# Attention and routed experts on one Trainium2 core: part of a weight split moved to GpSimd, routing temporaries in PSUM, masks in 64-row pieces, and a new order of the attention pass

## The chip, the cores and the metric

The kernel runs on one core of one Trainium2 chip. The core has five engines, each with its own in-order queue of instructions: TensorE (PE in the profile; PEld is its weight load), VectorE (DVE), ScalarE (ACT), GpSimd (POOL) and SyncE (SP, which here only issues transfers). Engines wait for one another through semaphores. Transfers between HBM and on-chip memory run on 16 DMA engines. The metric is the device time of one execution in microseconds, as the median of several runs.

## What is computed

Eight batches of eight heads go through two attentions whose results are added: one on queries, keys and values averaged in groups of four (then repeated four times), one local, in which a position sees its three neighbours on each side. The sums are the 4608 tokens of a mixture of eight experts: each token goes to the expert with the largest logit.

```python
out_d = sm_attn(q_d, k_d, v_d)                 # means of 4 positions
mask = np.abs(pos[:, None] - pos[None, :]) < 4
x = repeat(out_d, 4) + softmax(where(mask, scores, -1e9)) @ v
logits = x @ w_gate
expert_idx = np.argmax(logits, axis=1)
y = np.maximum(x @ w1[e], 0.0) @ w2[e]         # e = expert_idx of the token
out = softmax(logits)[expert_idx] * y
```

## The kernel before

**Attention.** 32 pairs of heads (NP = 32) go through a software pipeline. A list, `PASS` (L860), holds some fifty steps with a lag each; pass i (L878) calls each step in that order for pair i minus its lag, and each call appends its instructions to the engines' queues. So the list sets the order of work on every engine. In one pass stand, for different pairs: `pool_qk`, `pool_qk2`, `pool_v`, `pool_v2` (POOL, means of four); `s_loc` (PE: two matmuls that put the mask into PSUM, then 40 small score matmuls on 64x64 quarters of the array); `max_loc`, `sub_loc`, `sums`, `norm` (DVE) and `exp_loc` (ACT), the local softmax; `s_d`, `max_d`, `max_scale`, `exp_d`, `norm_d`, the same for the averaged attention; `t_loc`, `t_d` (PE transposes) and `e_loc`, `e_d` (ACT, their copies); `pv_loc`, `pv_d` (PE), `out_d` (ACT) and `add_up` (DVE), which write the token rows XT. The score bank pS, the bank pD and the output bank pPV have one buffer each; transposes rotate over three banks pX.

**Routing.** Every fourth pass closes a group of four or five tiles of 128 tokens. `ra_mm` (PE) and `ra_lg` (ACT copy) make its logits, the `rb_` steps (a PE turn, then small DVE and ACT operations) its expert and gate, the `rc_` steps its row in the sorted buffer xs in DRAM. `x_row` (L498: PE transposes, ACT copy into one of 7 slots) makes a tile's rows, and `x_out` (`scatter`, L525: a POOL memset and an indirect transfer) writes them into xs. Lags before: ra, rb and the first half of rc 4 (the same pass), x_row 4, the rest of rc and x_out 5.

**First weight.** In passes 15 to 30 `w1_hi` and `w1_lo` split 256 columns per pass of the first expert's w1 into a rounded high part (ACT, L177) and the rest (DVE, L179).

**Transition.** At the end of pass 31 `x_load(0, 0)` (L903) reads the first 256 rows of expert 0 back from xs, and the next three 512 KB weight blocks are requested. Then follow what is left of the pipeline (`steps(NP)` to `steps(NP + 3)`) with, between them, `route_b` of the last pair of batches (nine tiles, like each pair), `x_rows` for its tiles 2 and 3 (L911, L912), `prep` (turns and splits the rows read, L913) and the first expert matmuls (L915); the last groups' routing and scatters; and from L960 the loop over the experts, which the diff does not touch.

**Constants.** cb (identity, triangle, mask, bf16) and cf (f32) are issued on ACT's queue at the start; `pad_first` (L510) writes padding into xs in passes 3 and 4, and in pass 3 also the zero rows zs (L516).

## Time and profile before

| | before |
|---|---|
| runs (us) | 667.58, 667.40, 663.36; median 667.4 |
| profiled execution (us) | 670.7, span 668.9 |
| busy share of the span | PE 95%, DVE 54%, ACT 52%, POOL 33% |
| granted TensorE clock, mean | 0.98 of full speed |
| passes 0 to 31 and what is left of them | about 5 to 216 us of the span |
| experts | about 216 to 669 us |

The shares are means over two very different stages. In the expert stage PE is busy nearly all the time; in the attention stage DVE and ACT are busy some nine tenths as well. A row of the timeline reads: start in us from the start of the span, duration in us, engine, line, operation, output and inputs, count, and in brackets how long the engine stood idle before it and what ended the wait.

### The profile page before, as it was taken

How to read it: one execution, taken by the hardware profiler on the slowest of the kernel's cores; microseconds unless marked ns; L12 is line 12 of the kernel's file. 1: busy time of each engine (PE TensorE's matmuls, PEld its weight loads, DVE VectorE, ACT ScalarE, POOL GpSimd, SP SyncE). 2: the span in 40 equal slices, each digit the busy share in tenths (PEclk: the TensorE clock that was granted, in tenths of full speed). 3: DMA queues.
4: the chain of work that ended last, by engine and by line, in shares of the span. 5: the costliest groups of instructions: out<-in, count | busy, mean ns of one | idle time of the engine just before them, and what ended most of it. 6: DMA issues, size and time to landing. Idle time of an engine off the chain costs nothing.

```text
span 668.9 us, 15757 instructions
## 1 busy us (share of the span) xinstructions
PE 635.3 (95%) x6160; PEld 517.7 (77%) x6163; DVE 362.1 (54%) x715; ACT 347.6 (52%) x941; POOL 218.0 (33%) x324
## 2 busy tenths in 40 slices
PE   8799999999997989999999999999999989999994
PEld 4577777777775969888888888888888878888873
DVE  5868789999884537273274056157128238115020
ACT  4769799999995525362363254344236145224120
POOL 6765697798770611101101111101110101110111
PEclk9979999999998989999999999999999989999998
DMA  8987888988944388275266238328328528110001
GB/s 281 267 234 222 258 283 238 297 287 251 267 155 128 142 236 237 75 184 180 67 169 195 66 98 219 108 87 210 108 71 229 175 76 205 50 45 1 32 19 39
DMA packets 66227, 108.53 MB, mean 162 GB/s; under 512 B 15388, under 2 KB 36524, under 8 KB 66112
## 3 DMA queue, kind: packets, MB, share of 16 engines
q1 hardware_dynamic: 59840, 87.62, 46.9%
q0 software_dynamic: 5984, 19.01, 7.7%
q8 instruction: 66, 1.08, 0.7%
q10 hardware_dynamic: 288, 0.42, 0.2%
q14 instruction: 49, 0.40, 0.2%
HBM read 86.98 MB, written 23.67 MB: 165 GB/s over the span
## 4 chain that ended last, share of the span: by engine, by line
PE 77%; issue 10%; DMA 4%; POOL 4%; DVE 2%; ACT 1%; POOLq 0%; another core or an unknown queue 0%; SPq 0%; DVEq 0%; ACTq 0%
PE p L653 8%; PE p L652 8%; PE p L654 8%; PE p L666 7%; PE p L668 7%; PE p L667 7%; PE pD L286 3%; PE pPV L338 3%; PE pS L232 3%; PE pX L323 3%; PE pX L310 3%; PE pPV L351 3%; PE pX L748 2%; PE pX L767 2%; PE pX L501 2%
## 5 line engine op out<-in xcount | busy, mean ns | idle before, releaser
L652 PE MATMUL p<-xh,w1h 128*128 128x512 f32 (+1 forms) x288 | 107.6, 374 | 4.2 <-issue 2.0
L673 POOL DMA_INDIRECT out_dram<-y,tix x39 | 37.9, 973 | 217.0 <-ACT y L685 205.7
L653 PE MATMUL p<-xl,w1h 128*128 128x512 f32 (+1 forms) x288 | 107.0, 371 | 0.8 <-DVE xl L600 0.8
L654 PE MATMUL p<-xh,w1l 128*128 128x512 f32 (+1 forms) x288 | 106.7, 370 | 0.0
L666 PE MATMUL p<-w2h,hh 128*128 128x512 f32 x256 | 101.2, 395 | 0.0
L667 PE MATMUL p<-w2l,hh 128*128 128x512 f32 x256 | 99.7, 390 | 0.6 <-DVE w2l L642 0.6
L668 PE MATMUL p<-w2h,hl 128*128 128x512 f32 x256 | 99.8, 390 | 0.0
L657 DVE SCALAR_TENSOR_TENSOR hl<-p,hh 128x512 fp32r<-128x512 f32 (+1 forms) x72 | 45.5, 632 | 98.3 <-ACT hh L656 97.5
L656 ACT ACTIVATE hh<-p 128x512 fp32r<-128x512 f32 (+1 forms) x72 | 39.6, 551 | 82.0 <-PE p L654 81.0
L685 ACT ACTIVATE y<-p,gi 128x512 f32<-128x512 f32 x32 | 22.1, 689 | 94.2 <-PE p L668 89.8
L652 PEld LDWEIGHTS p<-xh,w1h 128*128 128x128 f32 x288 | 55.7, 193 | 14.5 <-issue 2.7
L653 PEld LDWEIGHTS p<-xl,w1h 128*128 128x128 f32 x288 | 55.6, 193 | 9.7 <-DVE xl L600 0.9
L654 PEld LDWEIGHTS p<-xh,w1l 128*128 128x128 f32 x288 | 55.6, 193 | 9.0
L667 PEld LDWEIGHTS p<-w2l,hh 128*128 128x128 f32 x256 | 48.1, 188 | 10.5 <-DVE w2l L642 1.0
L668 PEld LDWEIGHTS p<-w2h,hl 128*128 128x128 f32 x256 | 48.0, 188 | 10.3
L666 PEld LDWEIGHTS p<-w2h,hh 128*128 128x128 f32 x256 | 48.1, 188 | 9.4
L179 DVE TENSOR_TENSOR w1l<-raw,w1h 128x512 fp32r<-128x512 f32 (+1 forms) x72 | 51.3, 712 | 0.8
L642 DVE TENSOR_TENSOR w2l<-raw,w2h 128x512 fp32r<-128x512 f32 x64 | 43.4, 681 | 2.2 <-DMA xs<-xr,ix 1.5
L600 DVE TENSOR_TENSOR xl<-pX,xh 128x512 fp32r<-128x512 f32 x38 | 24.7, 684 | 35.2 <-ACT xh L599 34.2
L213 POOL TENSOR_TENSOR vdt<-vd 72x512 f32<-72x512 f32 x32 | 41.1, 1283 | 2.4
L177 ACT ACTIVATE w1h<-raw 128x512 fp32r<-128x512 f32 (+1 forms) x72 | 41.6, 578 | 0.0
L202 POOL TENSOR_TENSOR qkt<-qk 128x576 f32<-128x576 f32 x32 | 36.8, 1148 | 14.3 <-DMA qk<-in_qk_dram 12.2
(149 smaller groups left out, 1242.5 us busy)
## 6 DMA issues: line engine op xcount, KB each, us to landing
raw<-in_w_dram SPq DMA_DIRECT2D x64, 512.0 KB
qk<-in_qk_dram SPq DMA_DIRECT2D x32, 583.0 KB
vw<-in_vw_dram SPq DMA_DIRECT2D x32, 320.0 KB
vd<-in_vd_dram SPq DMA_DIRECT2D x32, 288.0 KB
xrow<-xs SPq DMA_DIRECT2D x32, 192.0 KB
xrow<-xs SPq DMA_DIRECT2D x32, 128.0 KB
xs<-zs SPq DMA_DIRECT2D x6, 512.0 KB
xs<-pad SPq DMA_DIRECT2D x3, 257.0 KB
```

Source lines behind the costliest of these rows:

```text
L177: nc.scalar.activation(hi[:, s], src[:, s], AF.Copy)
L179: nc.vector.tensor_sub(lo[:, s], src[:, s], hi[:, s])
L213: nc.gpsimd.tensor_add(t2, v[:, 0:2], v[:, 2:4])
L642: nc.vector.tensor_sub(lo, src, hi)
L652: nc.tensor.matmul(p, wh[:, fs], xh[:, k, r], start=(k == 0), stop=False)
L653: nc.tensor.matmul(p, wh[:, fs], xl[:, k, r], start=False, stop=False)
L654: nc.tensor.matmul(p, wl[:, fs], xh[:, k, r], start=False, stop=(k == 3))
L656: nc.scalar.activation(hh[:, f, r], p, AF.Relu)
L657: nc.vector.scalar_tensor_tensor(hl[:, f, r], p, 0.0, hh[:, f, r], op0=OP.max, op1=OP.subtract)
L666: nc.tensor.matmul(p, hh, wh, start=(f == 0), stop=False)
L667: nc.tensor.matmul(p, hh, wl, start=False, stop=False)
L668: nc.tensor.matmul(p, hl, wh, start=False, stop=(f == 7))
```

## The change

1. `w1_lo` runs on GpSimd instead of VectorE (only there; the experts' later splits stay on VectorE). `rc_run`, the addition to the running counts, also goes to GpSimd.
2. The routing temporaries rd and rs are columns of the PSUM bank that `rb_turn` wrote, not SBUF tiles.
3. The mask stands twice in the constants, for both halves of the rows, and `s_loc` writes it with four matmuls on 64x64 quarters instead of two on the full array. The mask is a tile and a transfer of its own, cf is issued after the second pair's q and k, its first use is after pass 2, and zs is written in pass 12.
4. `PASS` has a new order and new lags: rb 5, rc and x_out 6, x_row 5, s_d and max_d 1, exp_loc 1, pool_qk2 -1, pool_v2 0, eps and both inv 2, e_d and one half each of e_loc and t_d 3.

```diff
-B_END = B_MASK + NC * KW
+B_END = B_MASK + 2 * NC * KW
...
+    maskb = p1.tile([128, B_END - B_MASK], BF, name="mask", bufs=1)
+    nc.scalar.dma_start(maskb, csb[:, B_MASK:])
+    load_qk(1)
     cf = consts.tile([128, C_END], F32, name="cf")
     nc.scalar.dma_start(cf, cst)
-    load_qk(1)
...
-                nc.vector.tensor_sub(lo[:, s], src[:, s], hi[:, s])
+                (nc.vector if part is None else nc.gpsimd).tensor_sub(lo[:, s], src[:, s], hi[:, s])
...
-        for s in range(2):
-            nc.tensor.matmul(p[:, s * 512:s * 512 + NC * KW], identb, maskb, start=True, stop=False,
-                             skip_group_check=True)
+        for t in range(2):
+            for s in range(2):
+                r, o = slice((s ^ t) * 64, (s ^ t) * 64 + 64), s * NC * KW
+                nc.tensor.matmul(p[t * 64:t * 64 + 64, s * 512:s * 512 + NC * KW], identb[r, r], maskb[r, o:o + NC * KW],
+                                 start=True, stop=False, skip_group_check=True)
...
-        d = RS[m, "d"] = rp.tile([128, 5, E], F32, name="rd", bufs=1)
+        d = RS[m, "d"] = RS[m, "p"][:, 256:296].rearrange("p (t e) -> p t e", e=E)
...
-        sc = RS[m, "sc"] = rp.tile([128, 5, E], F32, name="rs", bufs=1)
+        sc = RS[m, "sc"] = RS[m, "p"][:, 320:360].rearrange("p (t e) -> p t e", e=E)
...
-        nc.vector.tensor_add(crun, crun, RS[m, "cs"])
+        nc.gpsimd.tensor_add(crun, crun, RS[m, "cs"])
...
-        if e == 0:
-            nc.sync.dma_start(zs, pad)
...
     PASS = (
-        (pool_qk2, 0), (norm, 2), (s_loc, 0), (w1_hi, 0), (ra_mm, 4), (max_loc, 0), (max_scale, 1),
...
+        (rb_turn, 5), (pool_qk, -1), (e_loc0, 3), (s_d, 1), (e_d0, 3), (rb_max, 5), (w1_hi, 0), (eps, 2),
...
+        if i == 2:
+            nc.vector.tensor_copy(crun, cf[:, C_CAP:C_CAP + E])
+        if i == 12:
+            nc.sync.dma_start(zs, pad)
```

On POOL, a pass of the weight split that is also a routing pass, before. The names: qkt, qkd and vdt, vds are the two steps of the means, ix the row numbers, xs<-xr the scatter.

```order
L202 TENSOR_TENSOR qkt<-qk 128x576
L219 TENSOR_TENSOR vds<-vdt 72x256
L213 TENSOR_TENSOR vdt<-vd 72x512
L475 CAST ix<-pos 128x5
L527 MEMSET spacer 1x1
L528 DMA xs<-xr,ix 42112x514
L208 TENSOR_TENSOR qkd<-qkt 128x288
```

And of the change (w1l is the low part of the weight):

```order
L207 TENSOR_TENSOR qkt<-qk 128x576
L218 TENSOR_TENSOR vdt<-vd 72x512
L213 TENSOR_TENSOR qkd<-qkt 128x288
L482 CAST ix<-pos 128x5
L467 TENSOR_TENSOR crun<-crun,cs 128x8
L224 TENSOR_TENSOR vds<-vdt 72x256
L532 MEMSET spacer 1x1
L533 DMA xs<-xr,ix 42112x514
L184 TENSOR_TENSOR w1l_2499<-raw,w1h_2498 128x256
```

Two instructions are new in the queue, and each second step of a mean now has another operation between it and its first step.

On DVE, a routing pass before: the routing chain (rm, rd, rs) stands between `sums` (L255) and `sub_loc` (L249) of the same pass in which its logits were made.

```order
L245 TENSOR_REDUCE mx<-pS 128x10
L255 TENSOR_REDUCE smd<-A 128x10
L405 TENSOR_REDUCE rm<-pX 128x5
L410 TENSOR_TENSOR rd<-pX,rm 128x40
L420 SCALAR_TENSOR_TENSOR rs<-rd,cf 128x40
L249 TENSOR_TENSOR A<-pS,mx 128x2x5x64
```

After the change that chain comes one pass later than the logits, early in the pass, and `sub_loc` directly follows `max_loc`.

On POOL at the transition, of the change, with what each instruction waits for (DMAHW are transfers issued by SP, DMASW those issued by POOL); the first row belongs to tile 6 of the third pair of batches, the second scatter to tile 7, the third to tile 8:

```order
L533 DMA xs<-xr,ix 42112x514 [waits Activation_49]
L532 MEMSET spacer 1x1 [waits Pool_49]
L533 DMA xs<-xr,ix 42112x514 [waits DMAHW2_49,DMAHW6_49,DMAHW1_49,DMAHW7_49,DMAHW0_49,Activation_49]
L532 MEMSET spacer 1x1 [waits Pool_49]
L533 DMA xs<-xr,ix 42112x514 [waits DMASW3_49,Activation_49]
L588 CAST tix<-gi 128x2
```

On ACT at the same place, of the change: the two copies of `x_rows` for tiles 2 and 3 of the last pair of batches, then the high parts xh of the rows read back.

```order
L449 ACTIVATE gt<-gt 128x4 [waits DVE_49]
L510 ACTIVATE xr<-pX 128x4x4x32 [waits DMASW1_49,PE_49]
L510 ACTIVATE xr<-pX 128x4x4x32 [waits DMASW2_49,PE_49]
L604 ACTIVATE xh_4462<-p_4464 128x4x128 [waits DMAHW4_49,DMAHW3_49,DMAHW5_49,DMAHW2_49,DMAHW6_49,DMAHW0_49,DMAHW7_49,DVE_49,Pool_49]
L604 ACTIVATE xh_4462<-p_4466 128x4x128 [waits DVE_49]
```

Before, the scatters of tiles 7 and 8 stood ahead of `x_load` in the program, and `x_load` waited for them. With lag 6 they stand behind it: it waits for tile 6 alone, and the scatter of tile 7 waits for its five reads (4 of rows, 1 of gates).

## Rows read from the trace of the kernel before

**Rows 1.** Table of stretches: from:to, length, busy time of PE, PEld, DVE, ACT, POOL with counts, granted clock, DMA share, GB/s. Passes 12 to 14; passes 16 to 21; the ten us after the first long wait of PE.

```profile
75.80:92.16 16.36, 15.44 (x354) 12.26 (x354) 14.86 (x37) 14.74 (x56) 10.01 (x15) 1.00 0.66 195
99.49:136.17 36.68, 35.05 (x770) 28.20 (x769) 33.37 (x80) 33.90 (x126) 29.25 (x39) 1.00 0.90 268
...
30.00:40.00 10.00, 6.97 (x67) 5.18 (x66) 3.46 (x9) 3.62 (x13) 6.32 (x7) 0.55 0.96 251
```

**Rows 2.** Timeline of DVE, `sub_loc` of passes 7, 10, 11, 15 and 31.

```profile
49.15 0.81 DVE L249 TENSOR_TENSOR A<-pS,mx 128x640 f32<-128x640 f32 x1
...
66.08 0.81 DVE L249 TENSOR_TENSOR A<-pS,mx 128x640 f32<-128x640 f32 x1
...
75.80 0.81 DVE L249 TENSOR_TENSOR A<-pS,mx 128x640 f32<-128x640 f32 x1
...
99.49 0.81 DVE L249 TENSOR_TENSOR A<-pS,mx 128x640 f32<-128x640 f32 x1
...
194.75 0.81 DVE L249 TENSOR_TENSOR A<-pS,mx 128x640 f32<-128x640 f32 x1
```

**Rows 3.** Timeline of ACT, the first `exp_d` of two passes of the weight split that follow each other, with no wait over 0.1 us between.

```profile
110.01 0.38 ACT L300 ACTIVATE AD<-pD,mxd 128x144 f32<-128x144 f32 x1
...
115.38 0.37 ACT L300 ACTIVATE AD<-pD,mxd 128x144 f32<-128x144 f32 x1
```

**Rows 4.** The chain that ended last, pieces on PE in passes 7 to 9: start, us, line, count. The ra_mm of a routing pass, and one pass without it, whose pieces follow without a gap from 53.40 to 58.55.

```profile
45.91 1.05 PE pX L384 x32
...
53.40 0.80 PE pPV L338 x37
...
55.55 0.33 PE pX L310 x3
...
57.56 0.27 PE pS L226 x2
57.84 0.71 PE pS L232 x40
```

**Rows 5.** The instructions of L179 up to 210 us: duration in ns, least, median, most, then the first and last start.

```profile
L179 DVE TENSOR_TENSOR w1l<-raw,w1h x16: 412/824/1105, 98.9 to 189.2; 128x256 fp32r<-128x256 f32 x16
```

**Rows 6.** Timeline of POOL: the start of its pass 15; row numbers and scatter of a routing pass; one pass without a wait; the second scatter of a pass with two; the start of its last full pass.

```profile
95.22 0.67 POOL L208 TENSOR_TENSOR qkd<-qkt 128x288 f32<-128x288 f32 x1
...
107.56 0.19 POOL L475 CAST ix<-pos 128x4 int32<-128x4 f32 x1 [1.99 <-DVE pos L470]
...
108.39 1.00 POOL L528 DMA_INDIRECT xs<-xr,ix  x1 [0.61 <-POOL spacer L527]
...
114.79 0.67 POOL L208 TENSOR_TENSOR qkd<-qkt 128x288 f32<-128x288 f32 x1
115.54 1.15 POOL L202 TENSOR_TENSOR qkt<-qk 128x576 f32<-128x576 f32 x1
116.65 0.73 POOL L219 TENSOR_TENSOR vds<-vdt 72x256 f32<-72x256 f32 x1
117.46 1.33 POOL L213 TENSOR_TENSOR vdt<-vd 72x512 f32<-72x512 f32 x1
...
118.98 0.99 POOL L528 DMA_INDIRECT xs<-xr,ix  x1 [0.15 <-issue]
120.00 0.67 POOL L208 TENSOR_TENSOR qkd<-qkt 128x288 f32<-128x288 f32 x1
...
149.21 0.96 POOL L528 DMA_INDIRECT xs<-xr,ix  x1 [0.21 <-issue]
...
192.31 0.68 POOL L208 TENSOR_TENSOR qkd<-qkt 128x288 f32<-128x288 f32 x1
```

**Rows 7.** Timelines of PE, ACT and DVE in pass 11, a routing pass.

```profile
71.89 0.60 PE L384 MATMUL pX<-XT,wgt 128*32 128x128 f32 x10 [0.97 <-issue]
...
72.52 0.38 ACT L391 ACTIVATE lg<-pX 128x256 f32<-128x256 f32 x1 [1.76 <-PE pX L384]
...
74.50 0.20 DVE L405 TENSOR_REDUCE rm<-pX 128x5 f32<-128x40 f32 x1 [2.97 <-PE pX L399]
```

**Rows 8.** Timelines of PE and of SP's issues around the first long wait of PE.

```profile
33.03 1.22 PE L338 MATMUL pPV<-AT,vw 64*64 64x58 f32 x34 [3.90 <-issue]
...
20.61 0.43 SPq L516 DMA_DIRECT2D zs<-pad  x1
```

**Rows 9.** Timelines at the transition: the last two-tile scatter on POOL, SP's issues, the turn on DVE, the gates' cast on POOL, the high parts on ACT, and the last pair's `add_up` on DVE.

```profile
196.50 0.96 POOL L528 DMA_INDIRECT xs<-xr,ix  x1 [0.21 <-issue]
...
201.67 1.82 SPq L564 DMA_DIRECT2D xrow<-xs  x4
203.54 0.46 SPq L576 DMA_DIRECT2D gi<-xs  x1
204.09 1.44 SPq L161 DMA_DIRECT2D raw<-in_w_dram  x3
...
206.27 1.32 DVE L595 STREAM_TRANSPOSE p<-xrow 128x512 f32<-128x512 f32 x2 [2.09 <-DMA xrow<-xs]
...
206.46 0.19 POOL L583 CAST tix<-gi 128x2 int32<-128x2 f32 x1 [8.24 <-DMA gi<-xs]
...
207.08 1.14 ACT L599 ACTIVATE xh<-p 128x512 fp32r<-128x512 f32 x2 [1.69 <-POOL tix L583]
...
214.96 0.83 DVE L366 TENSOR_TENSOR XT<-pPV,outd 128x290 f32<-128x290 f32 x2 [1.02 <-ACT outd L355]
```

More of the change, by code (lines that the diff above doesn't have):

```diff
@@ L69, in constants @@
         c_, t = divmod(g, 2)
-        b[t * 64:t * 64 + QB, B_MASK + c_ * KW:B_MASK + (c_ + 1) * KW] = m
+        for x in range(2):
+            o = B_MASK + (x * NC + c_) * KW
+            r = (t ^ x) * 64
+            b[r:r + QB, o:o + KW] = m
     c[:, C_TOK:C_TOK + NT] = np.arange(128)[:, None] + 128 * np.arange(NT)[None, :]
@@ L860, in attention_moe_kernel @@
     PASS = (
-        (pool_qk2, 0), (norm, 2), (s_loc, 0), (w1_hi, 0), (ra_mm, 4), (max_loc, 0), (max_scale, 1),
-        (norm_d, 2), (pv_loc, 3), (ra_lg, 4), (exp_d, 1), (rb_turn, 4), (pv_d, 3), (sums, 1), (rb_max, 4),
-        (t_d1, 2), (rb_sub, 4), (out_d, 3), (rc_run, 5), (w1_lo, 0), (rb_top, 4), (pool_qk, -1), (e_d1, 2),
-        (sub_loc, 0), (rb_first, 4), (add_up, 3), (rb_hot, 4), (rc_pos, 5), (t_d0, 2), (rb_eps, 5), (e_d0, 2),
-        (t_loc0, 2), (rb_exp, 4), (s_d, 0), (pool_v2, 1), (rc_last, 5), (pool_v, 0), (t_loc1, 2), (eps, 1),
-        (rc_ix, 5), (inv_d, 1), (e_loc0, 2), (x_out, 5), (exp_loc, 0), (rc_cs, 4), (e_loc1, 2), (rb_gate, 4),
-        (x_row, 4), (rc_place, 4), (inv, 1), (max_d, 0), (rc_rk, 4),
+        (rb_turn, 5), (pool_qk, -1), (e_loc0, 3), (s_d, 1), (e_d0, 3), (rb_max, 5), (w1_hi, 0), (eps, 2),
+        (rc_cs, 6), (t_d1, 3), (exp_loc, 1), (rb_sub, 5), (rb_exp, 5), (e_d1, 3), (rb_top, 5), (max_d, 1),
+        (rc_place, 6), (inv, 2), (rc_rk, 6), (max_scale, 1), (x_row, 5), (inv_d, 2), (rb_first, 5), (s_loc, 0),
+        (norm, 2), (rb_hot, 5), (rc_pos, 6), (norm_d, 2), (pool_v, 0), (max_loc, 0), (pool_qk2, -1),
+        (exp_d, 1), (pv_loc, 3), (rb_gate, 5), (rc_ix, 6), (pv_d, 3), (t_loc1, 2), (ra_mm, 4), (t_loc0, 2),
+        (out_d, 3), (sub_loc, 0), (e_loc1, 2), (rc_run, 6), (pool_v2, 0), (sums, 1), (rb_eps, 5), (rc_last, 6),
+        (t_d0, 2), (x_out, 6), (add_up, 3), (w1_lo, 0), (ra_lg, 4),
     )
@@ L873, in steps @@
                 f(i - lag)
-    nc.vector.tensor_copy(crun, cf[:, C_CAP:C_CAP + E])
     load_vd(0)
```

6 lines of the change are left out of this document (3 added, 3 removed).

## The prediction

> **What bounds the kernel now.** I read the table of stretches first. PE's 95% hides two stages: in the experts PE has no gaps and the diff does not touch a row there, so whatever changes must come from the attention passes and from the transition that follows them. In the attention stage no engine is alone: in passes 16 to 21 DVE is busy 33.4 and ACT 33.9 of 36.7 us, and DMA 0.90 of it [rows 1]. So I took the timelines of each engine, pass by pass. `sub_loc` on DVE marks the passes: passes 7 to 14 take 50.3 us (49.15 to 99.49), 9.7 of them pass 11; passes 15 to 30 take 95.3 [rows 2]. Three things hold them up. (a) The routing chain: in pass 11 PE's logits, ACT's copy, PE's turn and DVE's `rb_max` follow one another within one pass, and since `rb_max` stands ahead of `sub_loc`, ACT stands 1.76 and DVE 2.97 us; 0.97 of that began with PE itself waiting for nothing the profile shows [rows 7]. (b) In passes 15 to 30 the split on DVE: 0.41 us at best, 0.82 in the median, 1.1 at most, so it loses time beside POOL [rows 5]. (c) POOL is nearly full there too: a pass without a wait takes 5.21 us (114.79 to 120.00), and what it has to spare goes in waits for row numbers, 1.99 us in one [rows 6]. Earlier, PE stands 3.90 us in pass 5 [rows 8], and runs the ten us around and after it at a granted 0.55, for the most part the lower of its two levels [rows 1].
>
> At the end the way leads through POOL: its last scatter ends at 197.46, `x_load` is issued 4.2 us later, the rows are on chip 4.6 us after that, and ACT makes their high parts at 207.08 [rows 9]. The last pair's work waits behind them.
>
> **The change, part by part.**
>
> *Zero rows and constants.* zs is 128 x 514 x 4 bytes = 263 KB, which leaves the stretch where DMA is 0.96 busy at 251 GB/s [rows 1] and where PE's long wait lies, 12 us after zs was issued [rows 8]: 1.05 us of transfer, so what comes behind arrives about 1.0 us earlier. Where zs goes, around 80 us, DMA is busy 0.66 [rows 1], which covers it; without that cover it is 1.0 again. The mask adds 80 KB (0.3 us at that rate) to the start, under the first pair's q and k; cf later and crun after pass 2 are needed only by the routing. Taken as 0. **-1.0 us.**
>
> *Passes 7 to 14: the new order.* Logits, turn and rank now lie a pass apart, so (a) goes; what is late next is the fullest engine. ACT is busy 14.74 us in three passes, 4.9 each [rows 1]. PE's pieces of one pass follow each other for 5.15 us (53.40 to 58.55), and a routing pass adds 1.05 for the logits [rows 4], a quarter of that per pass, and I put 0.1 for turn and rank. Masks: two full-array matmuls take 0.27 us; the 40 score matmuls, on the same four quarters that the mask is to use, take 0.71, 18 ns for 64 columns of f32, where the full array takes 0.33 for 3 x 128 columns, 55 ns for 64 [rows 4]. So quarters run about three at a time, and four of 320 columns cost 0.27/2 x 4/3 = 0.18: 0.1 saved; the ends are 0.13 (all four together) and 0.54 (one by one). PE then needs 5.05 + 0.26 + 0.1 = 5.4, the fullest. 8 x 5.4 = 43.2 against 50.3 gives -7.1; I give back 0.6 because PE's own wait of 0.97 [rows 7] can return. **-6.5 us**; ends -8 (4.9 + 0.4 a pass) and -3.2 (only pass 11 returns to the mean of the others).
>
> The page TensorEngine Tiling (Array Packing) of the Trainium skill, section Restrictions and Gotchas, says that different row tiles cannot use one PSUM bank at the same time, and the new masks do send both halves of the rows to each bank. By it two quarters at most would overlap, the masks would cost 0.27 as before, and the sum would be 0.8 us worse. The score matmuls do the same and overlap, so the trace does not bear this out.
>
> *Passes 15 to 30: the low half on POOL.* DVE loses 16 times 0.82 us; that is covered, since ACT (5.37 us from one pass to the next, 110.01 to 115.38 [rows 3]) and POOL now set the pace. POOL before: 95.22 to 192.31 = 97.1 us for these 16 passes [rows 6]. After: a pass without a wait is 5.21; in it two second steps wait 0.08 for their first steps, where unrelated neighbours overlap by 0.04, and the new order puts another operation between both, 2 x 0.12 saved: 4.97. The low half has no row on POOL: 128 x 288 strided takes 0.67, in proportion 0.60 for 256; 72 x 256 contiguous 0.73; 128 x 576, more than twice as long, 1.15 [rows 6]. The first and the last are the ends; I take 0.73, same count and form, less 0.04 of overlap. 16 x 5.66 = 90.6, two second scatters 2.5 (0.96 + 0.21 + 0.09), and in four routing passes 0.12 for ix, 0.2 for the counts (about ix's 0.19) and 0.61 before the scatter, 3.7: 96.8. **-0.3 us**; by the ends -2.4 and +6.4. The waits for row numbers turn into work.
>
> The GPSIMD Engine Reference of the Trainium skill, section Key points, calls VectorE structurally about twice as fast on elementwise work. Twice the 0.41 of the undisturbed split would be 0.82 instead of 0.73, 1.4 us more in all, 665.4 instead of the time below. No row has this shape on POOL.
>
> *Pass 31 on POOL.* Before 192.31 to 197.46 = 5.15, with qkd and two scatters [rows 6, 9]; after vdt, vds and one scatter, 1.25 + 0.7 + 1.25 = 3.2. **-2.0 us.** `x_load` is thus issued 1.0 + 6.5 + 0.3 + 2.0 = 9.8 us earlier.
>
> *The transition: a new wait.* Before, ACT makes xh 5.4 us after `x_load` (201.67 to 207.08). Now the scatter of tile 7 waits for the five reads, and in ACT's queue the copy of tile 3 into the same slot, which waits for that scatter, stands ahead of xh. That is 4.8 us until the gates have landed (206.46), 1.0 on POOL, 4.2 for the transfer (as from 197.46 to 201.67; the weight blocks issued at 204.09 share the queue), 0.5 for the copy: 10.5 [rows 9]. **+5.1 us.** Queued behind it are all of ACT's steps for the last two pairs, on DVE the low parts, on PE the last transposes.
>
> *Behind xh.* From xh to the last `add_up` it takes 8.7 us before (207.08 to 215.80 [rows 9]). With e_loc0, both e_d and a transpose one step later, some four ACT copies of 0.3 us (nearest: 0.38 [rows 7]) come in front of the last outputs, part of them under the first expert matmuls: +1.0, between 0 and +2; the counts on POOL ahead of the last scatters +0.2. **+1.2 us.** Routing temporaries in PSUM: a bank is held until `rb_hot`, but its next user waits for `norm` just ahead of that; 0, at most one 0.2 us operation per routing pass, 1.4 in all.
>
> **Sum**: -1.0 - 6.5 - 0.3 - 2.0 + 5.1 + 1.2 = -3.5. The profiled execution goes from 670.7 to 667.2; it lies 3.3 above the median of the runs, which goes from 667.4 to **663.9**.
>
> **Rivals.**
> 1. PE's long wait in pass 5 goes as well. For it: zs stood just ahead of the transfers that run late there. Against: the other padding and the loads stay, and DMA is still full. It would save the 3.9 us, and at a granted 0.55 with 6.97 us busy in ten [rows 1, 8] about 0.45 x 7 = 3.1; less the 1.0 already counted, and 0.5 since the next pair's q and k limit: 663.9 - 5.5 = 658.4.
> 2. Slower: POOL sets the end and the low half costs its upper end, 1.15. Then 16 x 0.42 = 6.7 us come on top: 670.6. It passes the time before from 0.73 + 3.5/16 = 0.95 on. For it: POOL has no spare time in these passes, and `x_load` hangs on its queue. Against: the two nearest rows in size [rows 6].
> 3. The order does not do what it should: passes 7 to 14 keep the pace that they have apart from pass 11. The gain there is 3.2 instead of 6.5: 667.2, no change. For it: one-buffered banks (pS, pD, pPV) tie DVE, PE and ACT in rings. Against: with the new lags most handovers go to the next pass.
>
> **How the numbers follow.** My sum 0.42, its own range 660 to 668 from the ends of the mask, the transition and what lies behind xh; rival 1 0.22; rival 2 0.14; rival 3 0.22. A measurement of this kernel tells about 1% from no change: faster is below 660.7, slower above 674.1. Faster: rival 1 and a fifth of my own case, 0.30. Slower: rival 2 where it meets rival 3 (670.6 + 3.3) or a longer wait at the transition, 0.12. Same: 0.58. The range 655 to 672 leaves out the upper part of rival 2 and the lower of rival 1.
>
> **What would show it.** Order: DVE's wait ahead of `rb_max` under 0.5 us and passes 7 to 14 near 5.4; if 5.8, rival 3. Split: L184 on POOL near 0.73, POOL without waits in passes 18 to 30, DVE idle about a fifth; the median tells rival 2. Masks: four in about 0.18. PE's first long wait about 1 us earlier at its end; if it is gone, rival 1. Transition: the scatter of tile 7 directly after the gates' landing, ACT idle some 5 us ahead of the copy of tile 3. If ACT does not stand there, the prediction is too high by up to 5 us; if POOL has waits in passes 18 to 30, the sum's POOL terms are not the ones that count.

## The result, and the profile after

| | before | after |
|---|---|---|
| median of 15 runs each (us) | 665.13 (662.20 to 668.13) | 672.31 (666.00 to 678.87) |
| ratio, with 95% interval | | 1.0087 (1.0057 to 1.0116) |
| profiled executions (us) | 670.7 | 678.4, and 674.1 in a second one |

The changed kernel is slower by 0.9%, where 663.9 us and no loss were forecast; 672.31 lies just above the range. Its runs scatter over 13 us, those of before over 6. Ratios here leave out runs in a disturbed state and medians do not, so the two can differ, most for the gap of 320 bytes below. The rows that follow are of the second profiled execution (run `a0_again`), since the first one took 6 us more than the median; where the first is shown, it is said. The two profiles, before and `a0_again`, differ by 3.5 us, the medians by 7.2: the profiled execution of before lies 5.6 us above the median of its 15 runs.

Two lines of its page, then the table of stretches from `sub_loc` to `sub_loc`, passes 7 to 14 and 15 to 30, of the kernel before and of the changed one (columns as in [rows 1]):

```profile
span 672.4 us, 15936 instructions
...
PE 632.3 (94%) x6227; PEld 515.4 (77%) x6227; DVE 352.2 (52%) x691; ACT 344.0 (51%) x941; POOL 225.7 (34%) x348
```

```profile
49.15:99.49 50.34, 47.53 (x1033) 37.67 (x1032) 41.34 (x97) 43.45 (x155) 35.53 (x48) 1.00 0.81 253
99.49:194.75 95.26, 91.55 (x2049) 73.48 (x2047) 88.48 (x203) 87.67 (x317) 78.94 (x102) 1.00 0.84 256
```

```profile
44.84:89.23 44.39, 42.55 (x1043) 35.23 (x1031) 39.45 (x93) 40.87 (x152) 33.43 (x45) 1.00 0.97 288
89.23:191.39 102.16, 91.92 (x2097) 75.05 (x2094) 79.65 (x185) 88.09 (x324) 89.39 (x125) 0.97 0.82 244
```

In passes 15 to 30 VectorE is relieved (79.7 us of work, 88.5 before) and POOL has taken over (89.4, 78.9 before). In passes 7 to 14 the DMA engines have gone from a share of 0.81 to 0.97. PE was busy 47.5 of 50.3 and 91.6 of 95.3 us before, 42.6 of 44.4 and 91.9 of 102.2 now: in passes 15 to 30 it has as much to do as before and stands idle 10.2 us instead of 3.7. The timeline of DVE, `sub_loc` (now L256) of passes 7, 15 and 31, against 49.15, 99.49 and 194.75 [rows 2]:

```profile
44.84 0.82 DVE L256 TENSOR_TENSOR A<-pS,mx 128x640 f32<-128x640 f32 x1
...
89.23 0.82 DVE L256 TENSOR_TENSOR A<-pS,mx 128x640 f32<-128x640 f32 x1
...
191.39 0.82 DVE L256 TENSOR_TENSOR A<-pS,mx 128x640 f32<-128x640 f32 x1
```

So 4.3 us are gained up to pass 7, 5.9 more in passes 7 to 14, and 6.9 are lost again in passes 15 to 30 (102.2 us against 95.3). At pass 31 the lead is 3.4 us.

**The transition.** Timelines of SP, POOL, ACT, PE and DVE (answers to [rows 9]): the reads of rows, the scatter of tile 7, the copies of tiles 2 and 3, xh, PE's next transposes, and the last `add_up`.

```profile
195.53 1.83 SPq L569 DMA_DIRECT2D xrow<-xs  x4
...
201.53 0.96 POOL L533 DMA_INDIRECT xs<-xr,ix  x1 [8.25 <-ACT gt L449]
...
201.77 0.60 ACT L510 ACTIVATE xr<-pX 128x512 f32<-128x512 f32 x1 [0.71 <-PE pX L508]
206.76 0.60 ACT L510 ACTIVATE xr<-pX 128x512 f32<-128x512 f32 x1 [4.39 <-DMA xs<-xr,ix]
207.25 1.08 ACT L604 ACTIVATE xh<-p 128x512 fp32r<-128x512 f32 x2
...
207.41 0.78 PE L330 MATMUL pX<-cf,AD 112*72 112x112 f32 x3 [3.87 <-ACT xr L510]
...
218.79 0.82 DVE L373 TENSOR_TENSOR XT<-pPV,outd 128x290 f32<-128x290 f32 x2 [1.96 <-ACT outd L362]
```

The read is issued 6.1 us earlier than before. Then ACT stands 4.39 us for the scatter of tile 7 out of the slot that the copy of tile 3 needs, and xh comes 11.7 us after the read, 5.4 before. From xh to the last `add_up` it takes 11.5 us, 7.9 before. The lead of 6.1 has become a lag of 3.8. The granted clock in that stretch, from the table of stretches:

```profile
200.00:205.00 5.00, 1.98 (x8) 1.21 (x8) 1.90 (x6) 0.85 (x3) 2.20 (x4) 0.61 1.02 387
205.00:210.00 5.00, 2.04 (x15) 1.32 (x19) 2.07 (x5) 2.71 (x8) 0.00 (x0) 0.50 0.09 30
210.00:215.00 5.00, 5.00 (x62) 4.47 (x59) 1.03 (x3) 2.17 (x6) 0.00 (x0) 0.52 0.00 0
```

PE was busy two fifths of 200 to 210 us. The granted clock fell within 200 to 205 us, and PE ran its next work at 0.5, the lower of its two levels.

**The experts.** From the last `add_up` to the end it takes 453.6 us (672.4 - 218.79), and 453.9 before. But the profile of before holds a stop of PE there that this one does not. Its row in PE's timeline, and the stretch of 515 to 565 us of before and then of after:

```profile
538.63 0.50 PE L652 MATMUL p<-xh,w1h 128*128 128x512 f32 x1 [1.99 <-issue]
```

```profile
515.00:565.00 50.00, 48.01 (x205) 39.26 (x204) 24.15 (x39) 19.44 (x36) 6.37 (x13) 0.97 0.56 161
```

```profile
515.00:565.00 50.00, 50.00 (x220) 41.09 (x220) 25.88 (x42) 22.38 (x42) 6.04 (x11) 1.00 0.65 167
```

Behind the stop the granted clock is lower for 3.4 us. Without both the experts have become slower, though the diff touches no row of theirs. Groups of PE by line and shape, 270 to 535 us (count, busy us, mean ns of one), before and after:

```profile
L666 PE MATMUL p<-w2h,hh 128*128 128x512 f32 x165 | 65.1, 395 | 0.0
L667 PE MATMUL p<-w2l,hh 128*128 128x512 f32 x165 | 64.2, 389 | 0.0
L652 PE MATMUL p<-xh,w1h 128*128 128x512 f32 x160 | 62.2, 389 | 0.0
```

```profile
L657 PE MATMUL p<-xh,w1h 128*128 128x512 f32 x160 | 62.8, 393 | 0.0
...
L671 PE MATMUL p<-w2h,hh 128*128 128x512 f32 x158 | 62.6, 396 | 0.0
L672 PE MATMUL p<-w2l,hh 128*128 128x512 f32 x158 | 61.7, 391 | 0.0
```

Four nanoseconds in 389 in the mean of w1, with no wait in any row. The mean mixes two kinds. The same line in the changed kernel, in an odd expert (281 to 322 us) and in the even one behind it (333 to 372 us):

```profile
L657 PE MATMUL p<-xh,w1h 128*128 128x512 f32 x32 | 12.6, 395 | 0.0
...
L657 PE MATMUL p<-xh,w1h 128*128 128x512 f32 x32 | 12.5, 389 | 0.0
```

These matmuls overlap in the rows, so their pace is read from start to start: 233.3 ns in an odd expert, 226.7 in an even one, and 226.7 in both before. The outputs' scatters show the same: between the same two of an odd expert 55.4 us passed before (358.25 to 413.61), 56.4 now; of an even one 51.7 and 52.0.

```profile
358.25 0.99 POOL L673 DMA_INDIRECT out_dram<-y,tix  x1 [4.27 <-ACT y L685]
...
413.61 0.99 POOL L673 DMA_INDIRECT out_dram<-y,tix  x1 [4.43 <-ACT y L685]
```

```profile
361.80 0.98 POOL L678 DMA_INDIRECT out_dram<-y,tix  x1 [4.31 <-ACT y L690]
...
418.24 0.98 POOL L678 DMA_INDIRECT out_dram<-y,tix  x1 [3.88 <-ACT y L690]
```

Four odd experts at 1.0 and three or four even ones at 0.3 are 4.9 to 5.2 us.

### The profile page after: what moved, and what is told of

It reads as the page before. It is cut to its first block, busy times and chain, and to the rows that moved or that the text cites. A ratio compares the mean times of both kernels' runs of the same rounds, so it can differ in the third digit from the quotient of the medians.

```text
span 676.7 us, 15933 instructions
## 1 busy us (share of the span) xinstructions
PE 630.7 (93%) x6224; PEld 515.4 (76%) x6227; DVE 351.6 (52%) x691; ACT 343.9 (51%) x941; POOL 226.2 (33%) x348
## 3 DMA queue, kind: packets, MB, share of 16 engines
q1 hardware_dynamic: 59840, 87.62, 46.8%
## 4 chain that ended last, share of the span: by engine, by line
PE 67%; issue 10%; DMA 9%; POOL 7%; ACT 2%; DVE 1%; SPq 1%; POOLq 0%; another core or an unknown queue 0%; ACTq 0%; DVEq 0%
PE p L658 8%; PE p L659 8%; PE p L657 8%; PE p L673 7%; PE p L671 7%; PE p L672 7%; DMA xs<-xr,ix 6%; PE pD L293 2%; POOL xs L533 2%; POOL vdt L218 2%; PE pX L317 2%; PE pX L330 2%; PE pX L772 2%; PE pX L753 2%; PE pPV L345 2%
## 5 line engine op out<-in xcount | busy, mean ns | idle before, releaser
L662 DVE SCALAR_TENSOR_TENSOR hl<-p,hh 128x512 fp32r<-128x512 f32 (+1 forms) x72 | 45.5, 632 | 95.8 <-ACT hh L661 95.3
L657 PEld LDWEIGHTS p<-xh,w1h 128*128 128x128 f32 x288 | 55.3, 192 | 11.6 <-ACT xh L604 1.5
L533 POOL DMA_INDIRECT xs<-xr,ix x36 | 36.5, 1014 | 30.8 <-ACT gt L449 8.1
L184 DVE TENSOR_TENSOR w1l<-raw,w1h 128x512 fp32r<-128x512 f32 x56 | 39.5, 705 | 0.8
```

The source lines that it names most:

```text
L533: ins = nc.gpsimd.indirect_dma_start(out=xs, out_offset=bass.IndirectOffsetOnAxis(ap=IDX[m, t], axis=0), in_=xr, in_offset=None)
L657: nc.tensor.matmul(p, wh[:, fs], xh[:, k, r], start=(k == 0), stop=False)
L662: nc.vector.scalar_tensor_tensor(hl[:, f, r], p, 0.0, hh[:, f, r], op0=OP.max, op1=OP.subtract)
```

## Experiments

All are edits of the changed kernel unless said otherwise. Medians of before drifted between 662.5 and 665.1 us over the groups of runs, so the ratio to before on the same chip (95% interval) is the figure to compare. The columns in us are of each run's one profile: `sub_loc` of pass 7 to that of pass 31, read of rows to xh, xh to the last `add_up`; the last column is the mean w1 matmul of odd and even experts in ns.

| run | edit | median us | ratio to before | 7 to 31 | read to xh | xh to last add_up | w1 ns |
|---|---|---|---|---|---|---|---|
| before | | | | 145.6 | 5.4 | 7.9 | 389 |
| a0_again | none | 672.25 | 1.0100 (1.0060, 1.0139) | 146.5 | 11.7 | 11.5 | 393 |
| e1_out_ahead | tiles 7, 8 scattered ahead of the read | 674.12 | 1.0122 (1.0087, 1.0157) | 145.1 | 9.0 | 11.0 | 393 |
| e2_nine | nine slots | 665.83 | 1.0023 (0.9986, 1.0059) | 145.5 | 8.4 | 11.7 | 393 |
| e3_old_order | old list of the pass | 670.31 | 1.0083 (1.0056, 1.0111) | 146.5 | 6.0 | 8.2 | 393 |
| f1_after_cb | cb at its old size | 668.15 | 1.0033 (0.9996, 1.0070) | 146.6 | 12.3 | 11.9 | 389 |
| f2_before_cb | before, mask out of cb | 674.75 | 1.0124 (1.0074, 1.0174) | 145.1 | 5.4 | 8.5 | 393 |
| f3_rows_later | nine slots, rows 2, 3 later | 668.23 | 1.0035 (1.0003, 1.0067) | 144.0 | 5.9 | 15.3 | 393 |
| f4_right_gap | nine slots, gap of 640 B | 662.12 | 0.9963 (0.9924, 1.0002) | 151.3 | 8.1 | 12.2 | 389 |
| g1_low_dve | f4, low half on VectorE | 666.88 | 1.0064 (1.0041, 1.0087) | 147.6 | 8.5 | 12.0 | 389 |
| g2_zeros_early | f4, zero rows in pass 3 | 659.74 | 0.9963 (0.9933, 0.9993) | 144.4 | 7.5 | 12.0 | 389 |
| g3_temps_sbuf | f4, temporaries in SBUF | 659.77 | 0.9949 (0.9924, 0.9974) | 142.2 | 6.3 | 12.3 | 389 |
| g4_drain | f4, old lags after pass 31 | 662.05 | 0.9990 (0.9962, 1.0017) | 139.0 | 8.4 | 10.4 | 389 |
| h1_best | f4 with g2, g3, g4 and the counts on VectorE | 660.94 | 0.9973 (0.9940, 1.0006) | 155.3 | 7.8 | 10.7 | 389 |
| h2_half_values | f4, half of the value loads | 651.36 | 0.9807 (0.9757, 0.9856) | 146.4 | 9.0 | 11.6 | 390 |
| h3_gap_320 | nine slots, gap of 320 B | 669.62 | 0.9980 (0.9930, 1.0029) | 146.1 | 9.0 | 11.6 | 392 |
| h4_old_order_cb | old list, cb at its old size | 663.83 | 1.0009 (0.9980, 1.0038) | 147.5 | 6.7 | 9.2 | 389 |

### The slots, the transition and the list

> The changed kernel once more, unaltered, as the base of the next three on the same chip. Median near 672.3 us, between 666 and 679 as in the runs seen. Its profile should again show the ACT copy of the token numbers (L490) waiting for a scatter every fourth pass, most of it (4.7 us in the first profile) near 80 us, and ACT's high parts xh some 12 us after the first read of rows is issued.

The median is the same, and the waits are smaller or gone. ACT's copy of the token numbers (L490) in the second profile, and in the first one, with what PE then waited for there (ACT and PE timelines):

```profile
80.47 0.20 ACT L490 COPY xr<-cf 128x5 f32<-128x5 f32 x1 [1.83 <-DMA xs<-xr,ix]
```

```profile
84.27 0.20 ACT L490 COPY xr<-cf 128x5 f32<-128x5 f32 x1 [4.71 <-DMA xs<-xr,ix]
...
84.88 1.11 PE L508 MATMUL pX<-cf,XT 128*128 128x128 f32 x4 [4.13 <-ACT AT L324]
```

The copy writes into the slots from which the last group's last tile is still being scattered. Of two executions of one program one, of 678.4 us, loses 4.7 us there and the other 1.8. This wait near 80 us stands in all six profiles with seven slots and the zero rows in pass 12 (1.2 to 4.7 us), with the new list or the old one, and in neither of the two with the zero rows in pass 3 (before, f2). In `a0_again` the zero rows are issued at 67.36 us and the scatter that ends the wait at 72.88. That the one delays the other was not tried alone.

```diff
+            x_out(NP - 6)
             x_load(0, 0)
...
-            if 0 <= i - lag < NP:
+            if 0 <= i - lag < NP and not (i == NP and f is x_out):
```

> The scatters of tiles 7 and 8 of the third pair of batches stand ahead of the first read of rows again, the rest as in the change. Theory (a wait at the transition, from the slots and the lag of the scatter): the read is issued some 2.5 us later (two scatters of 1.0 with 0.25 around each on POOL), but xh comes 5.4 us after it instead of 11.9: 672.3 - 6.5 + 2.5 = 668.3 us. Rival (the last two pairs' own work, or the low granted clock there, sets the end, and ACT's wait lies beside it): 671 to 673. The waits in the passes (L490) are the same by both.

No gain, as the rival has it. The wait for tile 7 went, the read came 2.3 us later in the pass (6.4 us after `sub_loc` of pass 31, 4.1 in `a0_again`), and still xh took 9.0 us from it, not 5.4. So the slot's wait was not alone in front of xh.

```diff
-NX = 7
+NX = 9
...
-        return t if t < 4 else t - 4 if m < B // 2 - 1 else t - 9 + NX
+        return t
```

> Nine slots for the rows that are scattered instead of seven, a slot for each tile of a pair of batches, the rest as in the change. Theory (waits for slots): neither the copy of the token numbers in the passes nor the copy of tile 3 at the transition waits for a scatter. In the passes ACT's waits of 4.7, 2.0, 1.5 and 0.2 us go (8.4 in all, of which I count half to all), at the transition 6.5 us: 672.3 - 6.5 - 4.2 to 8.4 = 657.4 to 661.6 us, and the runs scatter less. Rival A (the DMA engines are the bound near 80 us, and the wait for the scatter only shows it): the wait comes back as one for q and k or for v, and only the transition's 6.5 are saved: 665.8. Rival B (neither wait sets the end): 671 to 673.

0.8% better than the change (1.0023 against 1.0100). At the transition xh comes 8.4 us after the read, 3.3 earlier than with seven slots. In the passes L490 waits for no scatter any more, yet `sub_loc` of passes 7 to 31 takes 145.5 us against 146.5: as rival A said, the passes do not get shorter by it, though no wait for loads has taken its place (2.5 us on POOL from 42 to 190 us, 2.8 in `a0_again`). What stands ahead of xh now, in the timelines of DVE, PE and ACT of this run:

```profile
197.36 0.17 DVE L444 TENSOR_REDUCE gt<-re 128x4 f32<-128x32 f32 x1
...
197.59 0.63 PE L508 MATMUL pX<-cf,XT 128*128 128x128 f32 x4 [1.74 <-DVE gt L444]
198.91 1.11 PE L508 MATMUL pX<-cf,XT 128*128 128x128 f32 x4 [0.69 <-ACT xr L510]
200.71 0.78 PE L330 MATMUL pX<-cf,AD 112*72 112x112 f32 x3 [0.69 <-ACT xr L510]
...
200.06 0.60 ACT L510 ACTIVATE xr<-pX 128x512 f32<-128x512 f32 x1 [1.20 <-PE pX L508]
200.55 1.08 ACT L604 ACTIVATE xh<-p 128x512 fp32r<-128x512 f32 x2
```

PE makes the rows of tile 2 when the routing chain is through, those of tile 3 when tile 2 is copied, and its next transposes when tile 3 is copied: one PSUM bank of three goes around. The other two hold t_loc0 and t_d0 of the last pass, which the new lags copy out a pass later.

> Nine slots as in the run before (665.8 us), and the rows of tiles 2 and 3 of the last pair of batches are made behind the next piece of the pipeline instead of ahead of it. In the run with nine slots xh came 8.4 us after the read of rows (5.4 before the change): two transposes and their copies in a row on one of the three PSUM banks, since the new lags keep two banks filled over the end of a pass. Theory (that row of copies holds xh, and with it the last two pairs): xh about 2 us earlier and the last add_up as much: 664 us. Rival (the last pairs' own chain with a pass more of it behind xh, and the low granted clock there, set the end): within 0.7 of 665.8.

```diff
-    x_rows(m, 2)
-    x_rows(m, 3)
     prep(0, 0, 1, get=h_bank)
     steps(NP + 1)
+    x_rows(m, 2)
+    x_rows(m, 3)
```

xh comes 5.9 us after the read, the theory's number, and the end is later, not earlier: from xh to the last `add_up` it takes 15.3 us. xh was held by that row of copies, but the end is set by the chain of the last pairs behind it. The ratio is within 0.12% of that with nine slots, so the rival was right.

> The list of the pass as before the change, with all its other edits (low half on POOL, temporaries in PSUM, masks in quarters, zero rows in pass 12). Theory (the order has brought both the gain of passes 0 to 14 and the two waits): without it POOL's passes 15 to 30 take 5.21 + 0.73 = 5.94 us, with the four routing passes and two second scatters about 101 against 97.1 before, 4 more, and masks and zero rows give back some 1.5: 665.1 + 2.5 = 667.6 us, with no wait of ACT for a scatter over 0.5 us. Rival (one of the other edits makes the loss, the order the gain): 672 or more, and the waits for scatters near 80 us stay.

It took the rival's side: 670.3, and the wait for a scatter near 80 us stays, so the new list has not brought it:

```profile
79.77 0.20 ACT L490 COPY xr<-cf 128x5 f32<-128x5 f32 x1 [1.95 <-DMA xs<-xr,ix]
```

The transition is nearly that of before (6.0 and 8.2), but the loss is still 0.8%. That points to the experts, where this run has no edit either and yet w1 matmuls of 393 ns. (Its rows give 396 and 397, but they hold a stop of 2.10 us at 328 us with 3.4 us of the lower granted clock behind it; the others are 392.5 in the mean.)

### The experts' matmuls

```diff
-    cb = consts.tile([128, B_MASK], BF, name="cb")
-    nc.scalar.dma_start(cb, csb[:, :B_MASK])
+    cb = consts.tile([128, B_MASK + NC * KW], BF, name="cb")
+    nc.scalar.dma_start(cb[:, :B_MASK], csb[:, :B_MASK])
```

> The change with one edit: the tile cb keeps the 640 bytes per partition that the mask took in it before (they stay empty), so that every tile that follows on the left side of the on-chip memory lies where it lay before. Seen so far: in the kernel before the expert matmuls of 512 columns take 389 ns, in the changed kernel 393 (w1) and 391 to 396 (w2), and between the same two outputs of two experts 55.4 us pass before and 56.4 after (odd experts), 51.7 and 52.0 (even ones). Theory (the place of the weights against the activations on chip sets the matmuls' pace): 389 ns again, 55.4 and 51.7, and about 4 x 1.0 + 3 x 0.3 = 4.9 us less than the changed kernel's 672.3: 667.4. Rival (the pace comes from what else runs, transfers or the clock, or differs from run to run): 392 to 396 ns stay and the time is 671 to 673.

The theory's numbers: 389 ns, 55.4 us for an odd expert (360.22 to 415.58), 4.1 us off the median. The same groups of PE as above, of this run:

```profile
L671 PE MATMUL p<-w2h,hh 128*128 128x512 f32 x164 | 64.8, 395 | 0.0
L672 PE MATMUL p<-w2l,hh 128*128 128x512 f32 x164 | 63.8, 389 | 0.0
L657 PE MATMUL p<-xh,w1h 128*128 128x512 f32 x160 | 62.2, 389 | 0.0
```

From the last `add_up` to the end it takes 448.7 us instead of 453.6, and from the first scatter of an output 425.6 instead of 430.6. Nothing but 640 empty bytes per partition differs.

```diff
-    cb = consts.tile([128, B_END], BF, name="cb")
-    nc.scalar.dma_start(cb, csb)
+    cb = consts.tile([128, B_MASK], BF, name="cb")
+    nc.scalar.dma_start(cb, csb[:, :B_MASK])
+    maskb = p1.tile([128, B_END - B_MASK], BF, name="mask", bufs=1)
+    nc.scalar.dma_start(maskb, csb[:, B_MASK:])
...
```

> The kernel before with one edit: the mask is a tile of its own in the pool of the attention passes, and cb is 640 bytes per partition smaller. Nothing else of the change. Theory (place on chip): the experts' matmuls go from 389 to 392 to 396 ns, 664.5 + 4.9 = 669.4 us, and the attention passes stay as they are. Rival: 389 ns and 664 to 665.5 us.

The kernel before takes on the slow matmuls with that edit:

```profile
L654 PE MATMUL p<-xh,w1h 128*128 128x512 f32 x160 | 62.8, 393 | 0.0
```

It loses 1.2%, more than 4.9 us. Some of the rest is at the start, where the mask comes as a transfer of its own ahead of cf and the second pair (first masks at 6.68 us, 5.35 before); the remainder is not explained.

```diff
+    _, gap = pool(name="gap", bufs=1, side="right")
+    nc.gpsimd.memset(gap.tile([128, NC * KW // 2], F32, name="hole"), 0.0)
     _, mp[1] = pool(name="m2", bufs=1, side="right")
```

> Nine slots, and an empty tile of 640 bytes per partition on the right side ahead of the tiles of the experts there (odd experts' w1, the last two blocks of w2, outputs), so that left and right tiles have the distance that they had before the change, while neither lies at its old place. Theory A (the distance between weights and activations counts): 389 ns and 55.4 us per odd expert, 665.8 - 4.9 = 660.9 us. Theory B (each tile's own place counts): odd experts stay at 56.4 or change otherwise, 664 to 668. Rival (pace is not from the places): 665.8 and 392 to 396 ns, as in the run with nine slots.

Theory A: 389 ns and 55.4 us (359.70 to 415.06), with the left tiles still at their new places:

```profile
L657 PE MATMUL p<-xh,w1h 128*128 128x512 f32 x160 | 62.3, 389 | 0.0
```

With the left tiles alone 640 bytes off the pace is the slow one, with both sides off it is that of before. So what counts is not the place of either but the distance between the tiles on the left (activations xh, most of w2) and those on the right (odd experts' w1). The ratio went from 1.0023 to 0.9963.

> Nine slots, and a gap of 320 bytes on the right instead of 640. Theory 1 (only the former distance of weights and activations gives the short matmuls): 392 to 396 ns and 56.4 us per odd expert as without a gap, 665.8 us, 1.0023 of the kernel before. Theory 2 (a part of the distance gives a part, or each distance has its own pace): 389 to 392 ns, 662 to 665 us.

Theory 1: 392 ns, and 56.5 us per odd expert (353.4 to 409.9); their w1 matmuls start every 233.3 ns, as without a gap. Half the distance gives nothing. The ratio's interval is wide, so no more than the pace is read from this run.

> The change with the old list of the pass, as in an earlier run (670.3 us, 1.0083 of the kernel before), and with the 640 bytes in cb again. It has all edits but the new order and the shift on chip. Theory (the shift cost 4.9 us of the experts in every kernel that has it, and the other edits come to about nothing): 665.4 us, 1.001 of the kernel before, so that the new order with seven slots (668.15 us with the same bytes in cb) costs the rest, 2 to 3 us. Rival (the other edits lose time in the old order, above all the low half on POOL): 668 us or more, and the new order costs nothing.

The theory again: 1.0009 instead of 1.0083, 389 ns. The change with its old list and its old places is level with the kernel before: the other edits come to nothing measurable. The new list with seven slots (f1, 1.0033) costs some 0.2% on top, within its interval; the profile of this run holds a stop of 2.08 us in the experts that f1's does not.

### Single terms, on the base f4 (nine slots, gap of 640 bytes)

```diff
-                (nc.vector if part is None else nc.gpsimd).tensor_sub(lo[:, s], src[:, s], hi[:, s])
+                nc.vector.tensor_sub(lo[:, s], src[:, s], hi[:, s])
```

> Base: nine slots and the gap of 640 bytes on the right (662.1 us). One edit: the low half of the weight's split stays on VectorE. Theory (POOL sets the pace of passes 15 to 30: a pass without a wait takes it 5.60 us there, 4.91 without the split): those passes take some 95 us as before the change instead of 98 and more, 662.1 - 3 = 659 us. Rival 1 (the split on POOL helps, since it slows VectorE by 16 x 0.8 us when it is there): 664 to 667. Rival 2 (neither engine sets the pace there; PE's waits for nothing that the profile shows do): 661.5 to 662.7.

Rival 1: 1.0064 against 0.9963. In this order the split on POOL is worth 1%: whatever POOL's full queue costs, 16 subtractions on VectorE cost more.

> Same base (662.1 us). One edit: the zero rows are written in pass 3 again, behind the padding of expert 0, not in pass 12. Theory (263 KB cost about 1 us wherever the DMA engines are full, and they are full at both places: shares of 1.02 at 20 to 30 us and 1.01 at 60 to 70): within 1 us of 662.1; PE's long wait near 32 us is 1 us longer, the waits between 70 and 85 us shorter. Rival (the move out of pass 3 was a gain): 663.5 or more. Rival (pass 12 is the worse place, because loads of q, k and the first weight come late behind it): 660 or less.

No difference (0.9963 both). With nine slots the place of the zero rows is worth nothing that can be told.

```diff
-RS[m, "p"][:, 256:296].rearrange("p (t e) -> p t e", e=E)
+rp.tile([128, 5, E], F32, name="rk", bufs=1)
...
-        ex = RS[m, "ex"] = rp.tile([128, 5, E], F32, name="re")
+        ex = RS[m, "ex"] = rp.tile([128, 5, E], F32, name="re", bufs=1)
...
-RS[m, "p"][:, 320:360].rearrange("p (t e) -> p t e", e=E)
+rp.tile([128, 5, E], F32, name="rs", bufs=1)
```

> Same base (662.1 us). One edit: the two routing temporaries are SBUF tiles again (one of them shares the tile of the ranks, for room). Theory (with both in one PSUM tile r_top on VectorE waits for the exponential on ScalarE, 0.3 to 1.0 us in each routing pass, 5.1 in all over eight, and the bank is held longer): that wait goes, of which a part shows: 658 to 661. Rival (that wait lies beside PE, which is the fullest engine): 661.5 to 662.7.

The wait of r_top (L427) for the exponential is gone, and xh comes 6.3 us after the read instead of 8.1: PE's wait ahead of the first of these rows is 0.69 us, ended by the difference rk, where it was 1.75, ended by the gate at the end of the chain, so the one free bank comes back earlier. The ratio, 0.9949, is the best of all and beats the kernel before (0.9924 to 0.9974), but its distance from the base is within the intervals.

```diff
+    AHEAD = (e_loc0, e_d0, t_d1, e_d1, pv_loc, pv_d)
...
+        if NP <= i < NP + 2:
+            for f in AHEAD:
+                f(i - 2)
```

(and the same steps skipped a pass later)

> Same base (662.1 us). One edit: for the last two pairs the steps that the new list puts one pass later (first copies of transposes, second transposes and copies of the averaged attention) and their output matmuls are issued in the pass of the old lags, ahead of the routing and the rows of the last pair of batches. Theory (what is left of the pipeline behind pass 31 is one chain through one or two free PSUM banks, part of it at the lower granted clock; from the read of rows to the last add_up it takes 20.9 us with nine slots and 14.1 before the change): 4 to 6 us of that come back, 656 to 658 us. Rival (the low granted clock after the wait for the rows takes it all again): 661 to 663.

The rival, by the ratio. In the profile, of an execution of 651.6 us, the shortest of all of this kernel, the chain behind xh is 1.9 us shorter and xh no earlier; PE runs at a granted 0.50 from 195 to 200 us there too.

> All that helped or did no harm on the base of nine slots and the gap of 640 bytes: temporaries in SBUF, zero rows in pass 3, the last two pairs drained with the old lags, and the running counts on VectorE again (in two profiles PE waits 1.1 and 1.6 us for POOL's addition to them before the count of tokens in pass 29). Theory (the single edits add up: 0.996 of the kernel before for the base, 0.1% for the temporaries, about 2 us from the drain by its profile, 1 us for the counts): 0.988 to 0.993 of the kernel before, 656 to 660 us. Rival (they save the same waits, or other waits take their place): 0.996, 661 to 662 us.

They do not add up: 0.9973.

> Base of nine slots and the gap of 640 bytes. The local values are loaded for every second pair only, and the next pair uses the same (so the output and the experts' counts are not the reference's, and only the passes' times are to be read): 16 loads of 320 KB, 5.2 MB, are left out. Open: between 20 and 195 us PE waits 10.4 us in waits of over half a microsecond for nothing that the profile shows, 4.9 in the kernel before (3.9 of them one wait), and in the stretches of 10 us the DMA engines' share reaches 1.01 and 1.02. Theory (these waits come where the DMA engines are full): they shrink to under 4 us, and from sub_loc of pass 7 to that of pass 31 it takes 140 us or less (151 in the base's profile, 145.6 before the change). Rival (they belong to places in the program, since L406 near 118, L330 near 137 and L317 near 156 us come back in several kernels): 6 us or more, 143 us or more.

The rival. PE's unnamed waits over half a microsecond come to 9.8 us, and passes 7 to 31 take 146.4. Rows of PE's timeline of `a0_again`, and the longest of this run:

```profile
153.07 0.91 PE L317 MATMUL pX<-cf,A 128*128 128x128 f32 x4 [1.96 <-issue]
...
166.75 1.73 PE L391 MATMUL pX<-XT,wgt 128*32 128x128 f32 x27 [1.71 <-issue]
```

```profile
174.83 0.48 PE L348 MATMUL pPV<-AT,vw 64*64 64x58 f32 x6 [3.02 <-issue]
```

They do not come from the amount that is loaded. What they wait for stays open. They go with the list: in passes 15 to 30 they come to 2.0 to 8.8 us in the fourteen profiles with the new list, and to 0.0 to 2.3 in the four with the old one (before, e3, f2, h4). The time of this run isn't comparable, since other counts of tokens reach the experts.

## Why the prediction was wrong

**The step that failed first: "the diff does not touch a row there, so whatever changes must come from the attention passes and from the transition".** The diff moves 640 bytes out of cb, everything behind it moves, and the experts take some 5 us more. f1, f4 and h4 undo it with one edit each (0.6% to 0.7% in their ratios to a0, e2 and e3), and f2 brings it into the kernel before; from the first scatter of an output to the end it is 430.6 against 425.6 us in a0 and f1, 428.8 against 423.6 in e2 and f4. The sum had no term for it, and no rival. Nor does PE have "no gaps" in the experts of before: there are the stop of 1.99 us and three waits of 0.6 to 1.5 us near 240 us.

**Passes 7 to 14, -6.5.** Mis-sized, and from one execution to the next not the same. In the six profiles with the new list that differ up to pass 31 in nothing but the slots and the size of cb (a0, e1, e2, f1, f3, h3; left out are after and f4, whose profiled executions took some 6 us more than their medians), they take 44.4 to 49.0 us, 46.8 in the mean, so -3.5. PE is busy 44.0 us of it in the mean, 5.5 a pass: what was late next was PE, as the prediction said, and its 5.4 a pass were right. What was too small are the 0.6 given back for PE's waits: PE stands 2.8 us idle in the mean, as long as before (50.34 - 47.53). The wait of VectorE ahead of `rb_max` for the group that pass 11 closes is 0.70 us in a0, 2.97 before. Rival 3, that the order does not reach its pace, was right in the mean, though its 3.2 is 3.9 by its own rows (9.72 for pass 11 less 5.80).

**Passes 15 to 30, -0.3.** The six profiles take 97.6 to 102.2 us, 98.8 in the mean, so +3.6. The step that failed is that POOL's work sets the pace: POOL is idle 10.4 us of them in the mean, which the prediction had named as the sign that its POOL terms do not count. What grew is PE's idle time, from 3.7 to 8.3 us in the mean. Waits of over half a microsecond for nothing that the profile shows make up 4.5 of it (8.1 in a0), none before. The wait ahead of `rb_max` comes back behind them (2.11, 1.29 and 4.23 us in a0). The temporaries in PSUM, put at 0 to 1.4 us, bring eight waits of r_top for the exponential, 4.4 us in a0; these and the waits for scatters can be taken away (g3, e2) without the passes getting shorter beyond their spread (142.2 and 145.5 us for both stretches). PE's own waits are not explained; that the new list brings them is read from profiles.

**Zero rows, -1.0.** Nothing measurable with nine slots (g2). The place was misread, too: they are issued at 67 us in a0, and from 65 to 75 us the DMA share before is 0.95 to 0.98, not 0.66, so nothing covers them. Yet pass 7 came 3.8 to 7.0 us earlier in those six profiles, about what rival 1 gave to PE's long wait: that was 2.15 us in a0 and 3.90 before [rows 8], with 3.4 us of the lower granted clock behind it instead of 10.2, so it got shorter and did not go. e3 and h4, with the old list, gained 2.5 there; the rest goes with the new list. This is read from profiles and was not tried alone.

**The low half on POOL.** Right in each number: 0.73 us each, no wait between the instructions of a pass, and a pass of 5.60 us (109.64 to 115.24) against 5.66 forecast. From the list of one line's instructions and the timeline of POOL of a0:

```profile
L184 POOL TENSOR_TENSOR w1l<-raw,w1h x16: 730/737/748, 92.3 to 189.2; 128x256 fp32r<-128x256 f32 x16
```

```profile
109.64 0.99 POOL L533 DMA_INDIRECT xs<-xr,ix  x1 [0.16 <-issue]
...
115.24 0.99 POOL L533 DMA_INDIRECT xs<-xr,ix  x1 [0.16 <-ACT AT L324]
```

But POOL was not the pace, since passes took 6.2 us each in the mean of the six. The upper end, rival 2, did not come. (The GPSIMD Engine Reference of the Trainium skill, section Key points, has VectorE about twice as fast: 0.737 against the undisturbed 0.41 of [rows 5] is 1.8 times, so the nearest row was the better price. By the rule 663.9 + 1.4 is 665.3, not 665.4.)

**Masks, -0.1 a pass.** Right in kind, and rather too small: from their start to that of the score matmuls four take 0.16 us, two took 0.37 before by the same reading, 0.27 by the chain's [rows 4]. All four start within 0.01 us (median). The timeline of PE, before and after:

```profile
57.40 0.43 PE L226 MATMUL pS<-cb 128*128 128x320 bf16 x2
57.77 0.79 PE L232 MATMUL pS<-qk 64*58 64x64 f32 x40
```

```profile
75.38 0.33 PE L233 MATMUL pS<-mask,cb 64*64 64x320 bf16 x4
75.54 0.73 PE L239 MATMUL pS<-qk 64*58 64x64 f32 x40
```

The rule of the Trainium skill's page TensorEngine Tiling (Array Packing), section Restrictions and Gotchas, that was weighed against it would have left the time as it was; this trace does not bear it out.

**Pass 31, -2.0.** Right, and a little more: the read is issued 4.1 us after `sub_loc` of pass 31 in a0, 4.7 in f1, 6.9 before.

**The transition, +5.1, and behind xh, +1.2.** Found, and too small: +6.3 and +3.7 in a0. Of the first, 3.3 us are the slot (e2); the other 3.0 are a mechanism that the prediction had costed at nothing: with lags that cross the end of a pass and temporaries that stay in PSUM, one bank of three is left when the pipeline drains (e2's rows; f3 takes 2.5 of it off xh, g3 1.8). Behind xh stand another pass's copies and matmuls, at the lower granted clock. e1, f3 and g4 show that taking one link out lets the next one set the end.

**The balance for a0**, against the profile of before: 4.3 us earlier at pass 7, 5.9 gained in passes 7 to 14, 6.9 lost in 15 to 30, 2.8 gained in pass 31, 6.3 + 3.7 lost at the transition, and the rest 0.3 less, with the stop of before in it: 672.4 - 668.9 = 3.5 (sums in hundredths). The prediction saw that the profiled execution of before lay above the median, and did not look where. The stop, with the lower clock behind it, hid most of the experts' loss in this comparison. But it is not shown to be that excess: the other three profiles with the old list hold such a stop as well (1.97 us in f2, 2.10 in e3, 2.08 in h4), and the executions of f2 and e3 lie at their medians (675.31 of 674.75, 670.33 of 670.31). Of the fourteen profiles with the new list one has one (h2, 2.31 us). So its going may be a gain of the change; what made the excess, and how much of the loss lies where in a median execution, stays open.
